# Early sums of the Fourier mixing moved ahead of the batch's end, and one operand of the two-level product formed a product earlier

## The chip, the cores and the metric

The kernel runs on one core of one Trainium2 chip, in fp32 throughout. The metric is the device time of one execution in microseconds (us). The engines are named as in the profile: PE is TensorE (matmuls and transposes), DVE is VectorE, ACT is ScalarE, POOL is GpSimd, SP issues most DMAs. PEld is the loading of weights, which runs beside the matmuls.

## The reference

Two blocks in a row. The first is attention over 8 batches x 8 heads, 576 positions, head size 64, in which only scores close to the row's maximum count:

```python
scores = scale * np.matmul(q, k.transpose(0, 1, 3, 2))
thresh = np.max(scores, axis=-1, keepdims=True) - tau
scores = np.where(scores >= thresh, scores, -1000000000.0)
attn = np.exp(scores - max); attn /= (sum + 1e-9)
x = attn @ v          # heads side by side: (8, 576, 512)
```

The second mixes every batch by a Fourier transform over both axes, keeps the real part, normalizes each row and runs it through two weight matrices:

```python
X = np.fft.fft(np.fft.fft(x, axis=1), axis=2)
u = x + np.real(X)
un = (u - mu) / np.sqrt(var + 1e-06)
ch = np.maximum(un @ w_ch1, 0.0) @ w_ch2     # 512 -> 2048 -> 512
return u + ch
```

## The kernel before

**Steps.** Attention goes by pairs of heads, four pairs to a batch, and by five query tiles to a pair, so a batch is 20 steps (`per_batch`) and the whole is 160. A step has scores on TensorE (L440, L446), the row maximum on DVE (`neg`, L520), the exponential on ACT (L526), a threshold (L530) and a masked sum on DVE (L540), and a scaling on ACT (L549). Transposes of the weights follow (`pe` L587, `pw` L605, copied from PSUM by ACT at L593 and L607), and products with v (`pv` L636, copied by ACT at L643). The loop over batches 2 to 7, which the change touches, starts at L1747 and writes out these pieces in a fixed order.

**Mixing.** The finished x of a batch is folded about its middle into `f` (L687 to L703; on DVE for the last pair, on POOL for the others). From the folds, sums and differences are formed that stand in for part of the transform. Some need only the first pairs of the batch: `fold_halves` (POOL) and `partial_sums` (DVE), a generator in three parts with 128 x 304 elements to an operation. Its first part is L729 and L730, its second part one `scaled` (L721) and its third two `scaled`. The rest is in `mixing(b)`, which the loop calls from step 2 of the next batch: the remaining sums (L751, L752, L754, L721), transforms over channels (`py` L766, copied by ACT into `y_e` and `y_o` at L771 and L776), transforms over positions (`pa` L783, L787) and additions into a ring of finished rows `u_t`.

The loop has `i` for the step. Before the change, at step 19 of a batch it creates the generator and runs its first part, behind the softmax's second third; it runs the second part further down in the same step. At the first step of the next batch it runs the third part, in the place where the first part stood. After the last step the third part stands behind the loop.

**Rows.** Finished rows go in nine groups of 512 through the two weight matrices. Group 0 is done plainly; groups 1 to 8 are `two_level(g, rows)`, a two-level Strassen scheme: seven products in place of eight, each of seven blocks. Its first half is `ph` (L1210) with sums on DVE (L1147) and ACT. Its second half has the products in the order `L1` = 1, 2, 5, 4, 6, 7, 3, at L1398, each in blocks `jn` 0 to 6. The left operands of the outer level are quadrants of the hidden layer (`a11`, `a12`, `a21`, `a22`) and combinations of them: product 1 reads `a11`, products 2 and 3 `a12`, product 5 and 6 `s1_tile`, product 4 `a22` and product 7 `a21`. Three of these are changed on the way by `l1_form`, in four parts of 128 x 512 at L1168: `a21 = a11 - a21` on POOL, `s1_tile -= a11` on DVE, and `a12 -= s1_tile` on POOL. The last one serves product 3, the last of the order, and reads the changed `s1_tile`.

The inner level needs four sums for each product, `l2_forms` (L1191): s1 and s2 on DVE, s3 and s4 on POOL, 128 x 512 each, formed while the product before runs. Product results come out of PSUM by an ACT copy (L1410) or a DVE addition (L1412, L1418), and are combined by POOL (`gather`, L1263) and DVE (`finish`, L895).

`at_slots(at, slots, jobs)` says behind which block `jn` of which product (index `at` in `L1`, from 0) a job is put on its engine's queue. Every engine runs its queue in order, and a job also waits for its inputs. While a softmax is being written out, such jobs are held back and follow it (`held`). `fill()` writes out as many blocks of the row groups as TensorE's budget for the step allows, so that products, attention and mixing lie beside each other. A group's rows are read back from `u_t` by `Rows.load` (`pn` L858, copies L863 and L864, statistics L869 and L870).

In the last group, 8, no attention runs any more. Its last two products are done plainly (L1377), and a `gather` addition of 128 x 896 on POOL (L1263) also lies behind block 1 of index 3.

PSUM is shared by all of this: four banks in a ring for everything but the scores (`po`, `ph`, `py`, `pa`, `pn`, `pe`, `pw`, `pv`) and two for the scores. A bank is free when its copy has run.

Of the kernel before, what the change touches and what calls it, by code (L numbers as in the profile page):

```python
# [47 lines left out]
def kernel(  # L48
# [378 lines left out]
    def scores(i):  # L427
        n, t = divmod(i, NT)
        qT, kT = heads[n][0:2]

        nh = 2 if t < 4 else 1
        sc = [ps.tile([128, 2, 512], FP32, tag="sc", name=f"sc{j}") for j in range(nh)]
        if t < 4:
            order = [(c, j) for c in range(2) for j in range(2)]
            if i < per_batch:
                order.sort(key=lambda cj: cj[1])
            for c, j in order:
                if True:
                    hp, k0 = slice(64 * j, 64 * j + 64), D * (1 - j)
                    nc.tensor.matmul(  # L440
                        sc[j][:, c, 0:HALF], qT[hp, 128 * t : 128 * t + 128],
                        kT[hp, k0 + HALF * c : k0 + HALF * (c + 1)], start=True, stop=True,
                    )
        else:
            for c in range(2):
                nc.tensor.matmul(  # L446
                    sc[0][:, c, 0:HALF], q_ends[:, :], kT[:, D + HALF * c : D + HALF * (c + 1)],
                    start=True, stop=True,
                )
        steps[i] = (sc, nh)  # L450
# [63 lines left out]
    def softmax_first(i):  # L514
        sc, nh = steps[i]
        neg = sb.tile([128, 2], FP32, tag="neg", bufs=3, name="neg")
        thr = sb.tile([128, 2], FP32, tag="thr", bufs=3, name="thr")
        e = sb.tile([128, 2 * S], FP32, tag="e", name="e")
        for j in range(nh):
            nc.vector.tensor_reduce(  # L520
                out=neg[:, j : j + 1], in_=sc[j][:, :, 0:HALF], axis=AXIS_XY, op=ALU.max,
                negate=True,
            )
        for j in range(nh):
            ej = e[:, S * j : S * (j + 1)].rearrange("p (c n) -> p c n", c=2)
            nc.scalar.activation(  # L526
                out=ej, in_=sc[j][:, :, 0:HALF], func=ACT.Exp, bias=neg[:, j : j + 1], scale=1.0
            )
            if j == 0:
                nc.scalar.activation(  # L530
                    out=thr[:, 0:nh], in_=neg[:, 0:nh], func=ACT.Identity,
                    bias=thr_off[:, :], scale=-1.0,
                )
        steps[i] = (sc, nh, e, thr)
# [185 lines left out]
    def scaled(out_, in0, factor, in1):  # L720
        nc.vector.scalar_tensor_tensor(  # L721
            out=out_, in0=in0, scalar=factor, in1=in1, op0=ALU.mult, op1=ALU.add
        )

    def partial_sums(b, eng=nc.vector):


        s = sums[b]
        eng.tensor_tensor(out=s[:, 0, E], in0=f[:, 0, E], in1=s[:, 1, E], op=ALU.add)  # L729
        eng.tensor_tensor(out=s[:, 0, O], in0=f[:, 0, O], in1=s[:, 1, O], op=ALU.subtract)  # L730
        yield
        scaled(s[:, 1, E], s[:, 1, E], flip, f[:, 0, E])
        yield
        scaled(f[:, 3, E], f[:, 3, E], minus, f[:, 0, E])
        scaled(f[:, 3, O], f[:, 0, O], plus, f[:, 3, O])
        yield
# [97 lines left out]
    def measure():  # L834
        while measures:
            measures.pop(0)()
# [257 lines left out]
    def quadrant(k, i):  # L1094
        return hs[:, 2048 * (2 * k + i) : 2048 * (2 * k + i + 1)]

    s1_tile = w1[3]
# [9 lines left out]
    def two_level(g, rows):  # L1107
# [52 lines left out]
        P, V = nc.gpsimd, nc.vector  # L1160
        a11, a12, a21, a22 = (quadrant(k, i) for i in range(2) for k in range(2))
# [3 lines left out]
        def l1_form(out_, in0, in1, engines):  # L1165
            def part(n, eng):
                c = slice(512 * n, 512 * n + 512)
                return lambda: eng.tensor_tensor(  # L1168
                    out=out_[:, c], in0=in0[:, c], in1=in1[:, c], op=ALU.subtract
                )  # L1170

            return [part(n, eng) for n, eng in enumerate(engines)]
# [97 lines left out]
        def gather(eng, v):  # L1270

            v = v.rearrange("p (j n) -> p j n", n=128)
            return [
                plus(eng, v[:, 1:5:3], twice(v[:, 0])),
                plus(eng, v[:, 5], v[:, 4]),
                plus(eng, v[:, 6], v[:, 2]),
                plus(eng, v[:, 6], v[:, 4]),
                plus(eng, v[:, 2:4], twice(v[:, 5])),
            ]
# [41 lines left out]
        def at_slots(at, slots, jobs):  # L1321
            for jn, job in zip(slots, jobs, strict=True):
                side.setdefault((at, jn), []).append(job)
# [12 lines left out]
        at_slots(1, (1, 2, 4, 6), l1_form(a21, a11, a21, (P, P, P, P)))  # L1336
        at_slots(2, (4, 5, 6), l1_form(s1_tile, s1_tile, a11, (V, V, V, V))[0:3])
        at_slots(3, (0,), l1_form(s1_tile, s1_tile, a11, (V, V, V, V))[3:4])
        at_slots(4, (1, 2, 4, 6), l1_form(a12, a12, s1_tile, (P, P, P, P)))
        at_slots(2, (0, 1, 2, 3, 4), gather(P, v_11))  # L1340
        at_slots(4, (2, 4), [lambda n=n: finish(0, 0, v_11)[n]() for n in range(2)])
        if not whole:
# [139 lines left out]
    per_batch = NPAIR * NT  # L1482
# [4 lines left out]
    def fill(hold=False, apart=False):  # L1487
        nonlocal budget, spent
        holding[:] = [True] if hold else []
        budget += per_slot  # L1490
        if mixes and not ended and not hold and not apart:
            mix(1)
        while work and spent < budget and work[0][0] < mixed:
            done = next(work[0][1], None)
            if done is None:
                work.pop(0)
            else:
                spent += done
        holding.clear()
        if mixes and ended:  # L1500
            mix(1)
# [124 lines left out]
    def fold_more():  # L1626
        if folds and next(folds[0], True):
            folds.pop(0)
# [16 lines left out]
    def mix(count):  # L1645
        nonlocal spent, mixed
        for _ in range(count):
            done = next(mixes[0], None)
            if done is None:
                mixes.pop(0)  # L1650
                mixed += 1
                break
            spent += done
# [93 lines left out]
    for i in range(2 * per_batch, total):  # L1747


        n, t = divmod(i, NT)  # L1750
        values = iter(())
        if i < total:
            scores(i)
        if t == 3 and i < total:
            values = values_in_parts(n, 0)
        elif t == 1 and n > 0:
            while folds:
                fold_more()
            values = values_in_parts(n - 1, 1)
        next(values, None)  # L1760
        if i % per_batch == 3:
            next(values, None)
        if i < total:
            softmax_first(i)
        next(values, None)
        if i % per_batch == 3:
            mix(1)
        if i % per_batch == 2:
            for _ in last_fold:
                pass  # L1770
            start_batch(i // per_batch - 1)
        fill(True)
        if i < total:
            softmax_second(i)
        measure()
        while held:
            held.pop(0)()
        if mixes:
            mix(1)
        if i % per_batch == 19:  # L1780
            partials = partial_sums(i // per_batch)
            next(partials)
        if i % per_batch == 0 and i > 2 * per_batch:
            next(partials)
        if t == 1:
            if n % NPAIR:
                folds.append(fold_rows(n - 1))
            else:
                last_fold = fold_rows(n - 1)
                next(last_fold)  # L1790
        weights = weights_in_parts(i - 1) if i <= total else iter(())
        next(weights, None)
        if t > 2 or i % per_batch == 17:
            fold_more()
        if i % per_batch == 19:
            next(partials)
        fill()
        if i % per_batch == 1:
            next(last_fold)
        next(weights, None)  # L1800
        if i < total:
            softmax_third(i)
            if t == 1:
                prep_ends(n)
            if t == 2 and n + 1 < B * NPAIR:
                scale_q(n + 1)
            if t == 3 and n + 1 < B * NPAIR:
                prep_pair(n + 1)
        if wanted:
            wanted.pop().factors()  # L1810
        if i % per_batch == 1:
            next(last_fold)
        fill(apart=i % per_batch == 2)
        if t == 2 and n + 1 < B * NPAIR:
            load_v(n + 1)
        if t == 4 and n + 2 < B * NPAIR:
            load_pair(n + 2)
    fill(True)
    while held:
        held.pop(0)()  # L1820
    next(partials)
    weights = weights_in_parts(total - 1)
    next(weights, None)
    fold_more()
# [83 lines left out]
```

## Time and profile before

| | us |
|---|---|
| median of 3 runs (1550.76 to 1551.69) | 1550.79 |
| profiled execution | 1552.55 |
| its span | 1550.8 |
| PE busy | 1523.1 (98%) |
| DVE busy | 1066.9 (69%) |
| ACT busy | 917.1 (59%) |
| POOL busy | 776.8 (50%) |

The span runs from the first instruction to the last; times in a timeline count from its start. A timeline line gives start, duration, engine, line, operation, output and inputs with their sizes, and after "x" the number of instructions of one kind drawn together; brackets at the end give the idle time before it and what ended it. The clock granted to TensorE was 1.00 over almost the whole span. The operations that the change moves, by their rows in the trace:

| line | engine | what | median, us | count |
|---|---|---|---|---|
| L729 | DVE | first early sum | 0.44 | 7 |
| L721 | DVE | scaled early sums | 0.53 | 32 |
| L1168 | POOL | a12 minus s1, one part | 1.34 | 32 |
| L1168 | DVE | s1 minus a11, one part | 0.68 | 32 |

The DVE part of L1168 stands at 470, 640, 810, 981, 1150, 1315, 1424 and 1519 us in groups 1 to 8, the a12 parts on POOL at 481, 650, 823, 992, 1162, 1327, 1432 and 1529.

### The profile page before, as it was taken

The numbers are of one execution on the slowest core, as the hardware profiler recorded it, in microseconds if no ns is written. First come the engines' busy times: TensorE is split into PE (matmuls) and PEld (weight loads), VectorE is DVE, ScalarE is ACT, GpSimd is POOL, SyncE is SP. The second block draws the span as 40 slices with busy tenths as digits, with TensorE's granted clock in tenths as the row PEclk, the third lists the DMA queues.
The fourth block names the chain that finished last, engine by engine and source line by source line (L and its number), as shares of the span: only waits on it lengthen the run. The fifth ranks groups of instructions, "written<-read, shape, count | busy, mean of one in ns | idle before, by whom it ended". The sixth has DMA issues, their size and how long they took to land.

```text
span 1550.8 us, 27036 instructions
## 1 busy us (share of the span) xinstructions
PE 1523.1 (98%) x9786; PEld 1185.1 (76%) x9786; DVE 1066.9 (69%) x2141; ACT 917.1 (59%) x1921; POOL 776.8 (50%) x964
## 2 busy tenths in 40 slices
PE   8999999999999999999999999999999999999999
PEld 5555555556788777877788778887788778989999
DVE  7987676846779466866588566956687666746546
ACT  6875675655656576656766666666666676232131
POOL 3775553034365643545254724555264626646635
PEclk9999999999999999999999999999999999999999
DMA  6423233465866344634464354635464534646655
GB/s 168 132 59 119 78 92 108 136 204 159 269 200 189 111 150 133 195 102 141 143 186 140 117 159 135 195 93 166 125 191 135 159 117 140 221 163 226 236 198 184
DMA packets 248907, 239.31 MB, mean 154 GB/s; under 512 B 197027, under 2 KB 218533, under 8 KB 228678
## 3 DMA queue, kind: packets, MB, share of 16 engines
q1 hardware_dynamic: 246262, 237.28, 50.1%
q8 instruction: 78, 1.28, 0.3%
q10 hardware_dynamic: 2512, 0.30, 0.1%
q14 instruction: 55, 0.45, 0.1%
HBM read 205.93 MB, written 31.46 MB: 153 GB/s over the span
## 4 chain that ended last, share of the span: by engine, by line
PE 84%; DVE 9%; ACT 3%; DMA 1%; POOL 1%; issue 1%; SPq 0%; ACTq 0%; DVEq 0%; POOLq 0%
PE ph L1210 25%; PE po L1398 18%; PE sc L440 9%; PE pv L636 9%; PE pw L605 7%; PE po L933 4%; PE ph L909 2%; PE sc L446 2%; PE py L766 2%; PE pa L783 1%; PE pe L587 1%; PE pa L787 1%; PE pm L360 1%; PE po L1377 1%; PE pn L858 1%
## 5 line engine op out<-in xcount | busy, mean ns | idle before, releaser
L520 DVE TENSOR_REDUCE neg<-sc 128x1 f32<-128x576 f32 x216 | 154.2, 750 | 113.0 <-PE sc L440 99.6
L526 ACT ACTIVATE e<-sc,neg 128x576 f32<-128x576 f32 x216 | 158.6, 734 | 121.6 <-DVE neg L520 121.5
L1147 DVE TENSOR_TENSOR hs<-ph,hs 128x512 f32<-128x512 f32 (+1 forms) x128 | 105.4, 823 | 168.0 <-PE ph L1210 97.7
L1398 PE MATMUL po<-w,w_all 128*128 128x128 f32 x1728 | 219.4, 276 | 0.3 <-ACT ends L593 0.3
L1398 PEld LDWEIGHTS po<-w,w_all 128*128 128x128 f32 x1728 | 205.0, 192 | 9.4 <-issue 4.0
L1156 POOL TENSOR_TENSOR w<-hs 128x512 f32<-128x512 f32 x32 | 42.1, 1317 | 313.8 <-ACT hs L1152 240.0
L540 DVE SCALAR_TENSOR_TENSOR e<-sc,thr,e 128x576 f32<-128x576 f32 x216 | 168.3, 812 | 20.6 <-ACT thr L530 20.6
L1210 PE MATMUL ph<-u_t,w 128*128 128x256 f32 x768 | 180.9, 382 | 0.5 <-DMA w<-f 0.5
L440 PE MATMUL sc<-kT,qT 64*128 64x288 f32 x1024 | 169.8, 431 | 7.1 <-DVE e L477 6.1
L607 ACT COPY e_t<-pw 128x512 f32<-128x512 f32 x256 | 148.6, 595 | 44.1 <-PE pw L605 42.7
L605 PE MATMUL pw<-ident,e 128*128 128x128 f32 x1152 | 168.8, 273 | 6.0 <-ACT ends L593 1.9
L549 ACT ACTIVATE e<-e,den 128x576 f32<-128x576 f32 x216 | 157.4, 775 | 8.9 <-DVE den L388 8.2
L1210 PEld LDWEIGHTS ph<-u_t,w 128*128 128x128 f32 x768 | 140.9, 190 | 23.6 <-issue 5.3
L1210 PE MATMUL ph<-w_all,w 128*128 128x256 f32 x672 | 157.1, 382 | 1.1 <-DVE w_all L1132 1.0
L605 PEld LDWEIGHTS pw<-ident,e 128*128 128x128 f32 x1152 | 134.8, 141 | 21.9 <-issue 5.6
L1152 ACT ACTIVATE hs<-hs 128x512 f32<-128x512 f32 (+1 forms) x96 | 74.1, 772 | 114.5 <-DVE hs L1147 113.7
L1210 PEld LDWEIGHTS ph<-w_all,w 128*128 128x128 f32 x672 | 123.4, 190 | 23.9 <-issue 4.9
L440 PEld LDWEIGHTS sc<-kT,qT 64*128 64x128 f32 x1024 | 96.3, 187 | 57.1 <-issue 23.7
L1263 POOL TENSOR_TENSOR w_all<-w_all 128x128 f32<-128x128 f32 (+2 forms) x160 | 118.4, 757 | 29.1 <-DVE w_all L1418 20.2
L1398 PE MATMUL po<-w,hs 128*128 128x128 f32 x912 | 120.0, 278 | 0.3 <-ACT ends L593 0.3
L1398 PEld LDWEIGHTS po<-w,hs 128*128 128x128 f32 x912 | 109.9, 192 | 9.9 <-issue 8.0
L593 ACT COPY ends<-pe 128x128 f32<-128x128 f32 (+1 forms) x128 | 38.1, 298 | 58.7 <-PE pe L587 40.1
(227 smaller groups left out, 2945.3 us busy)
## 6 DMA issues: line engine op xcount, KB each, us to landing
w<-f SPq DMA_DIRECT2D x150, 1024.0 KB, 4.9
hs<-in_moe_w_ch_dram SPq DMA_DIRECT2D x23, 512.0 KB, 4.7
q_in<-in_q_dram SPq DMA_DIRECT2D x128, 72.0 KB, 4.3
out_dram<-u SPq DMA_DIRECT2D x36, 256.0 KB, 2.5
k_in<-in_k_dram SPq DMA_DIRECT2D x124, 72.0 KB, 2.4
v_in<-in_v_dram SPq DMA_DIRECT2D x64, 128.0 KB, 5.0
f<-w SPq DMA_DIRECT2D x14, 512.0 KB, 3.3
f<-w SPq DMA_DIRECT2D x7, 1024.0 KB, 4.8
```

The lines of the kernel that those rows point to most:

```text
L440: nc.tensor.matmul(sc[j][:, c, 0:HALF], qT[hp, 128 * t : 128 * t + 128], kT[hp, k0 + HALF * c : k0 + HALF * (c + 1)], start=True, stop=True,)
L520: nc.vector.tensor_reduce(out=neg[:, j : j + 1], in_=sc[j][:, :, 0:HALF], axis=AXIS_XY, op=ALU.max, negate=True,)
L526: nc.scalar.activation(out=ej, in_=sc[j][:, :, 0:HALF], func=ACT.Exp, bias=neg[:, j : j + 1], scale=1.0)
L540: nc.vector.scalar_tensor_tensor(out=ej, in0=sc[j][:, :, 0:HALF], scalar=thr[:, j : j + 1], in1=ej, op0=ALU.is_ge, op1=ALU.mult, accum_out ...
L549: nc.scalar.activation(out=e[:, S * j : S * (j + 1)], in_=e[:, S * j : S * (j + 1)], func=ACT.Copy, scale=den[:, j : j + 1],)
L605: nc.tensor.transpose(pw[:, c, :], e[:, c0 : c0 + 128], ident[:, :])
L607: nc.scalar.copy(e_t[:, 4 * j : 4 * j + 4, qs], pw[:, :, :])
L636: nc.tensor.matmul(pv[64 * j : 64 * j + 64, 0:m], vt[:, 2 * c + j, :], e_t[:, 4 * j + c, 0:m] if c < 4 else ends[:, 0, 0:m], start=(c == 0 ...
L1147: nc.vector.tensor_tensor(out=to, in0=bank, in1=to if other is None else other, op=ALU.add)
L1210: nc.tensor.matmul(bank[:, 256 * q : 256 * q + 256].rearrange("p (two n) -> p two n", two=2), left[:, 256 * c + 128 * q : 256 * c + 128 * ...
L1263: return lambda: eng.tensor_tensor(out=to, in0=to, in1=other, op=ALU.add)
L1398: nc.tensor.matmul(to, lefts[m][j][:, s], right_[:, 128 * s : 128 * (s + 1)], start=jn in (0, 4) and s == 0, stop=s == 3, skip_group_check ...
```

## The change

The generator of early sums is created at the end of step 18, behind that step's last `fill`, and runs its first part there. In step 19 the place that was the first part's now runs the second (one `scaled`), and the place that was the second part's, just ahead of a `fill`, runs the third (two `scaled`), which stood in the first step of the next batch before. The call behind the loop goes. The four parts of `a12 -= s1_tile` go from behind blocks 1, 2, 4 and 6 of the fifth product in the order (index 4) to the same blocks of the fourth (index 3). The numbers of instructions on every engine and the order of TensorE's stay as they were. In the last group the first a12 part now stands on POOL's queue ahead of the 128 x 896 addition, the others between the fourth product's inner sums.

```diff
@@ -1336,7 +1336,7 @@
         at_slots(1, (1, 2, 4, 6), l1_form(a21, a11, a21, (P, P, P, P)))
         at_slots(2, (4, 5, 6), l1_form(s1_tile, s1_tile, a11, (V, V, V, V))[0:3])
         at_slots(3, (0,), l1_form(s1_tile, s1_tile, a11, (V, V, V, V))[3:4])
-        at_slots(4, (1, 2, 4, 6), l1_form(a12, a12, s1_tile, (P, P, P, P)))
+        at_slots(3, (1, 2, 4, 6), l1_form(a12, a12, s1_tile, (P, P, P, P)))
         at_slots(2, (0, 1, 2, 3, 4), gather(P, v_11))
         at_slots(4, (2, 4), [lambda n=n: finish(0, 0, v_11)[n]() for n in range(2)])
@@ -1778,9 +1778,6 @@
         if mixes:
             mix(1)
         if i % per_batch == 19:
-            partials = partial_sums(i // per_batch)
-            next(partials)
-        if i % per_batch == 0 and i > 2 * per_batch:
             next(partials)
         if t == 1:
             if n % NPAIR:
@@ -1811,6 +1808,9 @@
         if i % per_batch == 1:
             next(last_fold)
         fill(apart=i % per_batch == 2)
+        if i % per_batch == 18:
+            partials = partial_sums(i // per_batch)
+            next(partials)
         if t == 2 and n + 1 < B * NPAIR:
             load_v(n + 1)
@@ -1818,7 +1818,6 @@
     fill(True)
     while held:
         held.pop(0)()
-    next(partials)
     weights = weights_in_parts(total - 1)
```

## The prediction

> **What bounds the kernel now.** I read the busy shares first, then the chain that ended last, then TensorE's waits, then the timelines of the engines around the two places that the change touches.
>
> ```profile
> PE 1523.1 (98%) x9786; PEld 1185.1 (76%) x9786; DVE 1066.9 (69%) x2141; ACT 917.1 (59%) x1921; POOL 776.8 (50%) x964
> ...
> PE 84%; DVE 9%; ACT 3%; DMA 1%; POOL 1%; issue 1%; SPq 0%; ACTq 0%; DVEq 0%; POOLq 0%
> ```
>
> TensorE is busy 98% of the span. The change gives it no work and takes none, so time can only be won where it waits now, and lost where it would wait anew. Its waits between 800 and 1200 us, in us, number and longest:
>
> ```profile
> PE py L766 <- ACT y_e L776: 2.0, 3, 0.7
> PE pw L605 <- ACT w_all L1410: 1.5, 1, 1.5
> ```
>
> The three of 0.67 come after batch ends; smaller ones stand at 497.20 (0.19) and 656.35 (0.29), and one of 1.06 at 664.93, all behind DVE operations that wait for POOL's a12 parts. That is all I see to win: 3 x 0.67 + 0.19 + 0.29 + 1.06 = 3.55 us.
>
> Now VectorE (DVE) and then GpSimd (POOL) in one group's fourth and fifth product, about 981 to 1002 us:
>
> ```profile
> 981.25 0.66 DVE L1168 TENSOR_TENSOR w<-w,hs 128x512 f32<-128x512 f32 x1
> 981.82 0.97 DVE L721 SCALAR_TENSOR_TENSOR f<-f,factors 128x304 f32<-128x304 f32 x2
> 982.71 1.89 DVE L1168 TENSOR_TENSOR w<-w,hs 128x512 f32<-128x512 f32 x3
> 984.71 0.69 DVE L1191 TENSOR_TENSOR w_all<-w 128x512 f32<-128x512 f32 x1
> 985.31 1.42 DVE L520 TENSOR_REDUCE neg<-sc 128x1 f32<-128x576 f32 x2
> ...
> 991.89 3.14 DVE L692 TENSOR_TENSOR f<-half 128x143 f32<-128x143 f32 x4
> ...
> 997.47 1.77 DVE L1191 TENSOR_TENSOR w_all<-w_all,hs 128x512 f32<-128x512 f32 x1
> ```
>
> ```profile
> 987.14 1.32 POOL L1191 TENSOR_TENSOR w_all<-w 128x512 f32<-128x512 f32 x1 [7.94 <-PE po L1398]
> ...
> 992.14 2.72 POOL L1168 TENSOR_TENSOR hs<-hs,w 128x512 f32<-128x512 f32 x2
> 996.19 1.27 POOL L1191 TENSOR_TENSOR w_all<-hs 128x512 f32<-128x512 f32 x1 [1.33 <-PE po L1398]
> 997.42 1.28 POOL L1168 TENSOR_TENSOR hs<-hs,w 128x512 f32<-128x512 f32 x1
> ```
>
> The four L692 take 3.14 us in place of 4 x 0.30: two of them, beside POOL's L1168, take 1.37 each. L1191 at 997.47 takes 1.77 in place of 0.68, beside the L1168 at 997.42. L520, which reads PSUM, keeps its 0.75. So a DVE operation with two SBUF inputs waits out a POOL tensor_tensor (about 1.25 us from start to start), and the two engines then take turns. I count with that.
>
> **Place one: the early sums.** Per batch, L729 and L730 (0.44 and 0.47 us in five of seven batches) move from step 19 to the end of step 18; two L721 (0.89 us from start to start) move from the next batch's first step to step 19. Nothing is added in sum, and no DMA moves.
> - End of step 18, typical group (966 to 980): DVE comes free after the L1412 at 966.54, and POOL works without a gap from 965.25 to 970.46 (L1191, L1168 in turn). L729 and L730 each wait for one POOL operation, so the L520 at 968.84 starts about 0.86 late. What it feeds, e at L526, has TensorE work in front of it: no wait of PE.
> - Step 19: three L721 (3 x 0.445) replace L729, L730 and one L721 (1.19 from first start to last end). DVE's L1191 comes later by that and lets POOL's L1191 (released at 974.33) go ahead. At the L520 of 976.78 DVE is 0.8 late.
> - First step: 0.89 less before the L520 of 985.31.
> - First group (455 to 460): L729 before the L1412 of 457.31 makes that 1.0 later (L729 took 1.10 there, beside POOL). TensorE's L1398 at 458.10 waits for it: +1.0. In the third group (807.07) the existing wait of 1.52 grows by 0.97 for the same reason.
>
> **Place two: a12 during the fourth product.** Each of POOL's four a12 parts waits only for its own part of DVE's L1168 (s1 minus a11). Before, POOL was idle for 7.94 us up to 987.14 and took the parts from 992. Now the first part is released when the first DVE part ends, 0.6 us after 981.25, and DVE's other three are still to come. In turns: DVE's second part, POOL's first, DVE's third, POOL's second, DVE's fourth. Two DVE parts wait 1.25 each: +2.5. With 0.8 from place one and 0.89 saved, the L520 of 985.31 starts 2.42 late.
>
> Who waits for it? ACT runs in order:
>
> ```profile
> 986.16 0.74 ACT L526 ACTIVATE e<-sc,neg 128x576 f32<-128x576 f32 x1 [4.14 <-DVE neg L520]
> ...
> 987.61 0.42 ACT L643 COPY x<-pv 128x320 f32<-128x320 f32 x1
> ```
>
> ```profile
> 988.23 0.27 PE L587 MATMUL pe<-ident,e 128*128 128x128 f32 x1
> 988.34 0.60 PE L605 MATMUL pw<-ident,e 128*128 128x128 f32 x4
> ```
>
> The pv copy L643 is queued behind both exponentials and ends at 988.03. It empties one of the ring's four banks, and the pw at 988.34 takes that one. Slack 0.31. A start 2.42 later makes PE wait 2.1. The same order with the same slack stands at 646 (copy 645.96 + 0.42, pw 646.69) and at 1157 (1156.76, 1157.48). At 810 PE has already waited in front of this (slack 1.9): about +0.3 in all there with place one and less 0.67. In the groups without softmax (1316, 1424) no PE wait follows: GpSimd's fourth sum is due 0.6 us before it is needed.
>
> What the move frees: no a12 parts from 992 to 1002, some 3 us of waiting on DVE (two L692 1.08 each, L1191 1.1, L895). The later L721 and y_e come earlier, and the 3.55 us of old waits go.
>
> **The last group.** POOL, 1518 to 1535:
>
> ```profile
> 1522.04 2.53 POOL L1263 TENSOR_TENSOR w_all<-w_all 128x896 f32<-128x896 f32 x1
> 1524.53 1.72 POOL L1191 TENSOR_TENSOR w_all<-w 128x512 f32<-128x512 f32 x1
> 1527.76 1.27 POOL L1191 TENSOR_TENSOR w_all<-w,w_all 128x512 f32<-128x512 f32 x1 [1.51 <-DVE w_all L1191]
> 1528.98 6.19 POOL L1168 TENSOR_TENSOR hs<-hs,w 128x512 f32<-128x512 f32 x4
> ```
>
> Three a12 parts (1.25 each) now stand in front of the second L1191 (sum s4 for product 6), which ended at 1529.03. POOL's gap of 1.51 pays for some; DVE's two L1191 and its 896-wide L1263 take turns with the parts. Walked in turns, from 1522.6: a12 1523.85, DVE 1524.5, L1263 1526.5, DVE 1527.2, a12 1528.45, DVE 1529.1, L1191 1530.35, DVE 1531.4, a12 1532.7, L1191 about 1534.0. TensorE's blocks that read it start at 1531.79: +2.2, right at the end with nothing behind to take it up. No turn-taking: three parts less the gap leave it ready near 1531, no wait. These are the bounds, 0 and +2.3; I take the upper, as the L1168 of 1522.55 on DVE shows the same exclusion there (2.57 us beside L1263).
>
> **Sum**, us: first group +1.0 - 0.2 = +0.8; second +2.1 - 1.06 - 0.29 = +0.75; third +0.3; fourth +2.1 - 0.67 = +1.4; fifth the same +1.4; sixth and seventh 0; last +2.25. Total +6.9. The profiled execution took 1552.55 us, 1.76 above the median of the three runs; the sum on the median gives 1557.7.
>
> The wait at 985 is bounded below by 0 (POOL starts after DVE's fourth part) and above by 3.35: POOL's L1191 of 987.14, released by PE, and DVE's second L1191 start within 0.01 us of each other, and whichever comes second waits 1.25 more. I take 2.1, without that.
>
> The Trainium skill ("SBUF — State Buffer", the summary of rules for kernel authors) says that a DVE operation with two SBUF inputs and a GpSimd operation reading SBUF exclude each other fully, and that one should run whichever is off the critical path; that speaks against putting POOL's parts beside DVE's. Its section on the bandwidth intuition adds some 115 ns at a hand-over; estimated from that page, four hand-overs would make a group's delay 0.46 longer. The trace shows none: two alternating L692 start 1.30 apart, and POOL's operation is 1.24 to 1.28 of it.
>
> **The rivals.**
> - *Worse: a turn lost too.* At 987 POOL's L1191 gets in first in the second, fourth and fifth groups (3 x 1.25), and the y_e waits stay, their cause lying on ACT (3 x 0.67): 1557.7 + 3.75 + 2.0 = 1563.5. For it: the 0.01 us. Against: DVE's long rows just before each y_e wait.
> - *No change: L643 is not what pw waits for.* The bank is freed in time, PE keeps its order: 6.9 - 3 x 2.1 = +0.6, 1551.4. For it: the slack is read from one bank order and the trace names no such wait now. Against: pw starts 0.31 after the copy ends.
> - *Faster, the other side: these pairs don't exclude each other.* Parts of L1168 on both engines run side by side from 981.9, place one costs nothing, the last sum is ready at 1531, and DVE loses its company at 992: -3.55, 1547.2. It decides if DVE's L1168 keep under about 0.9 us on average. For it: L1168 of 982.71 and other DVE rows at full speed while POOL idles say nothing of it. Against: L692, L1191, L1168 at 1522.55 all stretched.
>
> **How the numbers follow.** Base case 0.52, worse 0.16, no change 0.14, faster 0.18. A difference of 0.2% (3.1 us) is about what a measurement here can tell. Range: low end 1549, which leaves out most of the faster case; high end 1563, which leaves out half of the worse one. Faster by over 3.1 us is 0.16 of the faster case's 0.18; within it, the no-change case's 0.14, 0.02 from faster and 0.03 from a base case whose tail bound is 0; the rest, 0.65, is slower.
>
> **What would show it.** Right: DVE's L1168 parts with a mean of 1.3 us or more; a PE wait "pw L605" behind L643's bank of about 2 at 647, 989 and 1159; a wait of L1398 for POOL's L1191 of about 2.2 near 1532; one of L1398 of 1.0 at 458; no y_e waits; L692 all at 0.3. Wrong: pw starting on time though the L520 is late; POOL's a12 parts beside DVE's with neither stretched; or, in the last group, a PE that does not wait.

## The result and the profile after

| | before | after |
|---|---|---|
| median of 8 runs, us | 1550.99 (1549.65 to 1554.14) | 1554.68 (1552.78 to 1557.31) |
| ratio to before | | 1.0023, 95% interval 1.0013 to 1.0034 |
| span of the profiled execution, us | 1550.8 | 1554.9 |
| PE / DVE / ACT / POOL busy, us | 1523.1 / 1066.9 / 917.1 / 776.8 | 1526.5 / 1076.5 / 914.2 / 786.1 |

The changed kernel is slower by 0.23%, 3.7 us; the forecast was 6.9. The runs of one kernel spread by some 5 us, and the long ones are those with the lower mean clock granted to TensorE: of 28 runs of the kernel before beside the first experiments, the three at 1.000 took 1549.1 to 1549.8 us, the ten at 0.998 1551.8 to 1553.8, the one at 0.996 1555.9. DVE and POOL show some 10 us more of busy time each with the same instructions: an operation that is held on its engine counts as busy (POOL's L1191 of 976.01 below shows 2.02 us in place of 1.27).

TensorE's waits over the whole run, after the change (us in all, times, longest), those that matter here:

```profile
PE pw L605 <- ACT x L643: 2.6, 3, 0.9
...
PE pw L605 <- ACT w_all L1410: 1.8, 1, 1.8
...
PE po L1398 <- POOL w_all L1191: 1.2, 1, 1.2
...
PE py L766 <- ACT y_e L776: 0.9, 5, 0.2
...
PE po L1398 <- DVE w_all L1412: 0.7, 1, 0.7
```

And the same view before, for the lines that differ past 450 us, where the changed code runs:

```profile
PE py L766 <- ACT y_e L776: 2.4, 5, 0.7
...
PE pw L605 <- ACT w_all L1410: 1.5, 1, 1.5
PE pw L605 <- DVE w_all L1418: 1.1, 1, 1.1
```

Three waits are new: for L643 (three times), for POOL's L1191 and for DVE's L1412, one each. One has grown, two have shrunk or gone. All were in the forecast; most are smaller than it said. Now the place around 983 us, on DVE, POOL, ACT and PE of the changed kernel:

```profile
976.21 0.69 DVE L1191 TENSOR_TENSOR w_all<-hs 128x512 f32<-128x512 f32 x1
...
978.50 1.41 DVE L520 TENSOR_REDUCE neg<-sc 128x1 f32<-128x576 f32 x2
...
982.95 4.62 DVE L1168 TENSOR_TENSOR w<-w,hs 128x512 f32<-128x512 f32 x4
987.67 0.69 DVE L1191 TENSOR_TENSOR w_all<-w 128x512 f32<-128x512 f32 x1
988.28 1.42 DVE L520 TENSOR_REDUCE neg<-sc 128x1 f32<-128x576 f32 x2
989.62 1.02 DVE L1191 TENSOR_TENSOR w_all<-w_all,w 128x512 f32<-128x512 f32 x1
```

```profile
976.01 2.02 POOL L1191 TENSOR_TENSOR w_all<-hs 128x512 f32<-128x512 f32 x1 [1.32 <-PE po L1398]
...
983.69 3.33 POOL L1168 TENSOR_TENSOR hs<-hs,w 128x512 f32<-128x512 f32 x2 [2.82 <-DVE w L1168]
```

```profile
989.13 0.74 ACT L526 ACTIVATE e<-sc,neg 128x576 f32<-128x576 f32 x1 [5.43 <-DVE neg L520]
...
990.58 0.42 ACT L643 COPY x<-pv 128x320 f32<-128x320 f32 x1
```

```profile
989.90 0.27 PE L587 MATMUL pe<-ident,e 128*128 128x128 f32 x1
991.05 0.66 PE L605 MATMUL pw<-ident,e 128*128 128x128 f32 x4 [0.88 <-ACT x L643]
```

DVE's four L1168 take 4.62 us where four at 0.60 from start to start and 0.08 more for the last one's end would be 2.5: two of them take 1.76 each, beside the two a12 parts that POOL starts at 983.69. The L520 behind them feeds the exponentials, L643 stands behind both, and pw starts 1.15 after the transpose L587 ahead of it; before, it was 0.11 (988.23 and 988.34). So 1.04 is lost here, and the same 1.04 at 649.60 and 1160.74.

TensorE runs the same 9786 matmuls and transposes in the same order in all kernels of this study, so each can be set against its counterpart and a loss be put on one instruction. From 450 us on, where the changed code runs, the changed kernel's order falls back by 3.19 us in its profiled execution; ahead of that, where no instruction of the change stands, the eleven other profiles end between 3.2 us earlier and 1.0 later than the kernel before.

### The profile page after: what moved, and what is told of

The parts are those of the page before. It is cut to its first block, busy times and chain, and to the rows that moved or that the text cites. A ratio compares the mean times of both kernels' runs of the same rounds, so it can differ in the third digit from the quotient of the medians.

```text
span 1554.9 us, 27021 instructions
## 1 busy us (share of the span) xinstructions
PE 1526.5 (98%) x9786; PEld 1186.0 (76%) x9786; DVE 1076.5 (69%) x2141; ACT 914.2 (59%) x1921; POOL 786.1 (51%) x964
## 4 chain that ended last, share of the span: by engine, by line
PE 86%; DVE 5%; ACT 3%; POOL 3%; issue 2%; DMA 0%; POOLq 0%; ACTq 0%; DVEq 0%
PE ph L1210 24%; PE po L1398 19%; PE pv L636 10%; PE sc L440 9%; PE pw L605 7%; PE po L933 4%; PE ph L909 3%; PE sc L446 2%; PE py L766 2%; PE pd L111 1%; PE pa L783 1%; PE pe L587 1%; PE pa L787 1%; PE pm L360 1%; PE po L1377 1%
## 5 line engine op out<-in xcount | busy, mean ns | idle before, releaser
L520 DVE TENSOR_REDUCE neg<-sc 128x1 f32<-128x576 f32 x216 | 154.2, 751 | 106.9 <-PE sc L440 99.6
L1398 PE MATMUL po<-w,w_all 128*128 128x128 f32 x1728 | 219.9, 277 | 2.2 <-POOL w_all L1191 1.2
L1398 PEld LDWEIGHTS po<-w,w_all 128*128 128x128 f32 x1728 | 205.1, 192 | 11.6 <-issue 4.5
L540 DVE SCALAR_TENSOR_TENSOR e<-sc,thr,e 128x576 f32<-128x576 f32 x216 | 168.3, 812 | 22.3 <-ACT thr L530 22.1
L1398 PE MATMUL po<-w,hs 128*128 128x128 f32 x912 | 120.0, 278 | 0.3 <-ACT ends L593 0.3
L1398 PEld LDWEIGHTS po<-w,hs 128*128 128x128 f32 x912 | 109.9, 192 | 9.9 <-issue 8.0
L1191 POOL TENSOR_TENSOR w_all<-hs 128x512 f32<-128x512 f32 x38 | 54.0, 1421 | 43.8 <-PE po L1398 43.7
```

The costliest lines, as they stand in the source:

```text
L520: nc.vector.tensor_reduce(out=neg[:, j : j + 1], in_=sc[j][:, :, 0:HALF], axis=AXIS_XY, op=ALU.max, negate=True,)
L540: nc.vector.scalar_tensor_tensor(out=ej, in0=sc[j][:, :, 0:HALF], scalar=thr[:, j : j + 1], in1=ej, op0=ALU.is_ge, op1=ALU.mult, accum_out ...
L1398: nc.tensor.matmul(to, lefts[m][j][:, s], right_[:, 128 * s : 128 * (s + 1)], start=jn in (0, 4) and s == 0, stop=s == 3, skip_group_check ...
```

## The experiments

Each kernel was run beside the kernel before on the same chip. "In the trace" means the shift of TensorE's order against the kernel before, from 450 us to the end, in one profiled execution each. A wait for a DMA at 1451 us (0.3 to 0.6 in these kernels) alone shifts it by up to 0.25 one way or the other.

**One part alone.** The sums as changed, a12 as before:

```diff
-        at_slots(3, (1, 2, 4, 6), l1_form(a12, a12, s1_tile, (P, P, P, P)))
+        at_slots(4, (1, 2, 4, 6), l1_form(a12, a12, s1_tile, (P, P, P, P)))
```

> The early sums as in the changed kernel, a12 during the fifth product as before. My theory: this part alone costs the late L1412 in the first group (0.84 us in the changed kernel's trace) and a little at 808 (0.24), and wins nothing: the waits of py for y_e stay at 0.67 and the one at 665 at 1.06, and there is no wait of pw for L643, since the L520 in question comes earlier, not later. About +1.1 us on the kernel before, 1552.1. Rival, the sums carry the whole loss: 1554 or more. Rival, the sums are hidden wholly: 1551.0.

Ratio to before 1.0007 (0.9998 to 1.0016); in the trace +1.07. The two steps are 0.84 at 457 and 0.25 at 808, and y_e's waits and the one at 665 are as before. By the trace the sums cost a microsecond and win nothing; the times alone do not tell this kernel from the one before.

And a12 as changed, the sums as before (the diff's first part alone):

> a12 during the fourth product as in the changed kernel, the early sums where they were before. My theory: the L520 behind DVE's L1168 parts starts 2.1 late and not 1.3, as the 0.89 us that the two L721 take away from in front of it are not saved; pw waits for L643 about 1.85 instead of 0.88, in three groups; the waits for y_e fall to 0.18, the one at 665 to 0.1, and the last group loses 1.4. Sum +5.5 - 1.5 - 1.0 + 1.4 = +4.4, 1555.4. Rival, the wait for L643 has nothing to do with where the L721 stand: 0.88 stays, and the whole is +1.6 to +2, 1552.8.

Ratio 1.0026 (1.0015 to 1.0038), about 4.0 us; in the trace +4.60. Its waits:

```profile
PE pw L605 <- ACT x L643: 5.0, 3, 1.7
...
PE po L1398 <- POOL w_all L1191: 1.2, 1, 1.2
...
PE py L766 <- ACT y_e L776: 0.9, 5, 0.2
```

The wait for L643 is 1.68 each and not 0.88 (1.84 in TensorE's order, against 1.04). So the two parts don't add: the sums' move takes 0.89 us from in front of that L520 and so halves the harm that the a12 move does there. Alone, it has nothing to halve.

**The last group.** The changed kernel with a12 at the old place in group 8 only:

```diff
-        at_slots(3, (1, 2, 4, 6), l1_form(a12, a12, s1_tile, (P, P, P, P)))
+        at_slots(4 if whole else 3, (1, 2, 4, 6), l1_form(a12, a12, s1_tile, (P, P, P, P)))
```

> The changed kernel, but in the last group a12 stands behind the fifth product again. My theory: only the wait of L1398 for POOL's L1191 near 1535 goes (1.2 us idle, 1.37 in TensorE's order), 1.4 us less than the changed kernel, 1553.3. Rival, something else ends the last group: time as in the changed kernel, 1554.7.

Ratio 1.0011 (1.0002 to 1.0020), against 1.0023 with the whole change. In the trace +1.88 against +3.19; the only step of more than 0.15 us in which its order differs from the changed kernel's past 450 us is that of L1398 in the last group, 1.37. That wait is the a12 parts' doing.

**The order on ACT.** The changed kernel with pv's copy ahead of the exponentials in the batch's second step:

```diff
-        if i % per_batch == 3:
+        if i % per_batch in (1, 3):
             next(values, None)
```

> The changed kernel, but in the second step of each batch the copy of pv (L643) is put on ACT ahead of the two exponentials instead of behind them. Nothing else moves. My theory: what L643 waits for is the queue: it now runs as soon as pv is done (by 988.1, before the row maximum), and pw starts on time; the three waits of 0.88 go, 1.04 each in TensorE's order, and 3.1 us with them: 1551.6. Rival, the wait passes to the next copy behind the exponentials (L1410), whose bank TensorE wants next: 1554.7.

Ratio 1.0012 (1.0003 to 1.0021); in the trace +2.52, so 0.7 better than the changed kernel and not 3.1. Both theories have a share. ACT and PE:

```profile
983.91 0.43 ACT L643 COPY x<-pv 128x320 f32<-128x320 f32 x1 [3.99 <-PE pv L636]
985.34 0.74 ACT L526 ACTIVATE e<-sc,neg 128x576 f32<-128x576 f32 x1 [1.00 <-DVE neg L520]
...
986.78 0.58 ACT L1410 COPY w_all<-po 128x512 f32<-128x512 f32 x1
```

```profile
986.12 0.27 PE L587 MATMUL pe<-ident,e 128*128 128x128 f32 x1
986.23 0.60 PE L605 MATMUL pw<-ident,e 128*128 128x128 f32 x4
987.42 2.05 PE L1398 MATMUL po<-w,w_all 128*128 128x128 f32 x16 [0.59 <-ACT w_all L1410]
```

L643 runs 1.4 us ahead of the first exponential, and pw starts on time (1.04 gone): the queue was what L643 waited for. But the next bank of the ring is emptied by L1410, which still stands behind the exponentials, and 0.76 of the 1.04 comes back half a microsecond later. That leaves 0.28 three times; 0.26 of it goes again in the second group, where py now waits for y_e. Moving one copy out of the queue does not mend it; the late L520 has to go.

**Earlier, but behind DVE's parts.** The kernel before with a12 in the fourth product at its end:

```diff
-        at_slots(4, (1, 2, 4, 6), l1_form(a12, a12, s1_tile, (P, P, P, P)))
+        at_slots(4 if whole else 3, (1, 2, 4, 6) if whole else (4, 5, 6, 6), l1_form(a12, a12, s1_tile, (P, P, P, P)))
```

> The kernel before, but in groups 1 to 7 the four a12 parts stand behind blocks 4, 5, 6 and 6 of the fourth product: still a product earlier than before, but on POOL's queue behind the inner sum s3, which waits for TensorE till past DVE's four L1168 parts. The last group and the early sums are as before. My theory: the harm of the earlier place is its meeting with DVE's L1168 ahead of the row maximum, not its being earlier. So DVE's parts stay at 0.68, no wait of pw for L643 comes up, and the wins stay: y_e 3 x 0.49 and most of 0.97 at 665. About -2.4 us on the kernel before, -0.15%. Rival, the wins of the changed kernel need POOL free by 988 and are lost here: 0. Second rival, any earlier a12 delays POOL's s4 and TensorE waits for it: slower, +1 or more.

Ratio 0.9992 (0.9983 to 1.0002); in the trace -1.86. No wait for L643, the three y_e waits down by 0.49 each, the one at 665 down by 0.97; 0.2 is lost again at 829 and 998 each, and some 0.7 near 1454. The direction is that of my theory; by its times alone this kernel is not told from the one before (its runs had a mean granted clock of 0.9977, those of the kernel before 0.9985, which by the spread above I estimate to be worth about 1 us).

The same with the changed sums:

> The same late place of a12 in groups 1 to 7 and the old one in the last group, with the early sums of the changed kernel. My theory: the sums cost their 0.84 in the first group and 0.25 at 808 here too and win nothing, so 1.1 us more than with the old sums: -1.3 us on the kernel before. Rival, with the L643 wait gone the two L721 taken out of the batch's first step pay: equal to or faster than with the old sums.

Ratio 1.0001 (0.9992 to 1.0010), in the trace +0.32. That is 2.2 more than with the old sums. The 0.84 and 0.24 are there, and a third, unforeseen, of 1.14 at 1168, where pw waits for L593. That copy stands behind the exponentials, and they wait for a late row maximum. What makes it late is a lost turn. DVE and POOL with the changed sums:

```profile
1158.76 2.99 DVE L687 TENSOR_TENSOR half<-x 128x287 f32<-128x287 f32 x2
...
1163.73 1.76 DVE L1191 TENSOR_TENSOR w_all<-hs 128x512 f32<-128x512 f32 x1
1165.41 1.41 DVE L520 TENSOR_REDUCE neg<-sc 128x1 f32<-128x576 f32 x2
```

```profile
1158.71 1.27 POOL L1191 TENSOR_TENSOR w_all<-w,w_all 128x512 f32<-128x512 f32 x1
```

and with the old ones:

```profile
1157.54 1.87 DVE L687 TENSOR_TENSOR half<-x 128x287 f32<-128x287 f32 x2
...
1161.40 1.75 DVE L1191 TENSOR_TENSOR w_all<-hs 128x512 f32<-128x512 f32 x1
1163.07 1.41 DVE L520 TENSOR_REDUCE neg<-sc 128x1 f32<-128x576 f32 x2
```

```profile
1157.55 1.55 POOL L1191 TENSOR_TENSOR w_all<-w,w_all 128x512 f32<-128x512 f32 x1
```

DVE's L1191 is held alike in both (1.76 and 1.75), so it is not the difference. The difference is L687: POOL's L1191 starts 0.05 us ahead of it with the changed sums and goes first, and 0.01 behind it with the old ones and goes second. In TensorE's order the L520 is 1.12 later for it. This 1.14 hangs on 0.06 us and came in one of three groups; whether every run has it is not shown.

**What excludes.** Three variants, each with POOL's a12 parts replaced in the changed kernel: by memsets of a12, by memsets of s1, and by copies.

```diff
-        at_slots(3, (1, 2, 4, 6), l1_form(a12, a12, s1_tile, (P, P, P, P)))
+        at_slots(3, (1, 2, 4, 6), [lambda n=n: P.memset(a12[:, 512 * n : 512 * n + 512], 0.0) for n in range(4)])
```

> The changed kernel, but POOL's four a12 parts are memsets of the same 128 x 512 pieces, in the same places: the subtraction of a12 is left out, so that product 3 has a zero operand. Theory: DVE's two-input L1168 is held because POOL's operation reads SBUF. Then all four DVE parts take 0.66 to 0.70, the row maximum behind them starts 2.1 earlier, and pw does not wait for L643. Rival, it is held by any POOL work on these tiles, writes too: two of four parts stay at 1.7 or at 0.68 plus the memset's own time, and the wait for L643 remains.

DVE's parts took 0.66 to 0.68 at 980 and no wait for L643 was left; in the trace -1.63 (one run, 1550.46). But here the two did not meet: the first two memsets need nothing of DVE and ran at 978.10 and 978.56, ahead of its first part at 980.24. At this place it says only that without the meeting there is no harm. Elsewhere in the same trace they do meet. The fourth memset runs beside DVE's four L692, which have two SBUF inputs too. DVE and POOL:

```profile
990.87 0.99 DVE L692 TENSOR_TENSOR f<-half 128x143 f32<-128x143 f32 x4
```

```profile
991.11 0.53 POOL L1339 MEMSET hs<- 128x512 f32 x1
```

None of the four is stretched (0.29 to 0.34 each; beside the subtraction two took 1.37 each in the kernel before). In the first, sixth and seventh group the second memset also ran beside one of DVE's L1168 (at 470.76, 1316.71 and 1425.57), and that one took 0.68. So a POOL operation that only writes does not hold DVE's.

```diff
+        at_slots(3, (1, 2, 4, 6), [lambda n=n: P.memset(s1_tile[:, 512 * n : 512 * n + 512], 0.0) for n in range(4)])
```

> The changed kernel, but each of POOL's four a12 parts is a memset of the part of s1_tile that DVE's L1168 has just written: it is released by the same DVE part, meets the next one as a12 did, and reads nothing. The subtraction of a12 is left out and product 6 has a zero operand. Theory, the exclusion needs a POOL operation that reads SBUF: all four DVE parts stay at 0.66 to 0.70, POOL's memsets at about 0.53, and pw does not wait for L643. Rival, any POOL access excludes: two DVE parts grow by a memset's 0.5, to about 1.2, or the memsets wait for DVE's parts to end.

This was to mend that and did not: the memset also waits until DVE's L1191 has read the part (it ran at 982.62, past all four L1168). TensorE then waited for the memsets in the last groups (4.9 us), so the one time, 1558.36, says nothing of the change. Beside L692 (its fourth memset, 990.17) the picture is the same as above: 0.29 to 0.34 each.

```diff
+        at_slots(3, (1, 2, 4, 6), [lambda n=n: P.tensor_copy(a12[:, 512 * n : 512 * n + 512], s1_tile[:, 512 * n : 512 * n + 512]) for n in range(4)])
```

> The changed kernel, but each of POOL's four a12 parts copies the part of s1_tile that DVE's L1168 has just written into a12: one operand read in place of two, the subtraction left out (product 3 reads s1 minus a11 there). Theory, one read is enough to exclude: two DVE parts take 0.68 plus the copy's own 0.6 or so, some 1.2 to 1.3, and pw waits for L643 by what that adds beyond the slack, 0 to 0.3. Rival, only two-input POOL operations exclude: DVE's parts stay at 0.68.

Here they met. DVE and POOL:

```profile
979.25 3.29 DVE L1168 TENSOR_TENSOR w<-w,hs 128x512 f32<-128x512 f32 x4
982.64 0.69 DVE L1191 TENSOR_TENSOR w_all<-w 128x512 f32<-128x512 f32 x1
983.25 1.41 DVE L520 TENSOR_REDUCE neg<-sc 128x1 f32<-128x576 f32 x2
```

```profile
979.97 2.02 POOL L1339 COPY hs<-w 128x512 f32<-128x512 f32 x2 [2.80 <-DVE w L1168]
```

Four parts in 3.29 us: two of them took 1.09, that is 0.41 more than 0.68. With the subtraction it was 1.07 more, with nothing beside it 0. So, with the memset's zero, it is POOL's reading that counts, one read is enough, and the wait grows with POOL's operation (a copy takes 0.60 alone, a subtraction 1.27). No wait for L643 was left, as the two turns lost (0.83) are what the moved sums save (0.89): the L520 at 983.25 is on time in TensorE's order. The trace is at -1.60 (one run, 1549.46).

**A version that beats both.** As with the late place above, but in groups 1 to 6 only:

```diff
-        at_slots(4, (1, 2, 4, 6), l1_form(a12, a12, s1_tile, (P, P, P, P)))
+        at_slots(4 if g > 6 else 3, (1, 2, 4, 6) if g > 6 else (4, 5, 6, 6), l1_form(a12, a12, s1_tile, (P, P, P, P)))
```

> The kernel before with a12 behind blocks 4, 5, 6 and 6 of the fourth product in groups 1 to 6 only; groups 7 and 8 and the early sums as before. In the trace with the late place to group 7, TensorE lost 0.5 near 1454 behind L1132, which the old place of group 7 does not. My theory: the wins stay (3 x 0.49 and 0.97) and this 0.5 does not come up: -2.4 us on the kernel before, ratio 0.9984, clear of 1. Rival: the 0.5 comes from elsewhere and stays, -2.0.

Median 1549.10, ratio 0.9985 (0.9976 to 0.9994): faster than before, by 2.3 us going by the ratio and by 1.7 going by the medians (1550.77 before); in the trace -2.22, and the loss near 1454 does not come up. POOL and DVE in the same stretch as above:

```profile
984.50 1.32 POOL L1191 TENSOR_TENSOR w_all<-w 128x512 f32<-128x512 f32 x1 [7.94 <-PE po L1398]
...
986.58 1.27 POOL L1168 TENSOR_TENSOR hs<-hs,w 128x512 f32<-128x512 f32 x1
```

```profile
980.07 1.89 DVE L1168 TENSOR_TENSOR w<-w,hs 128x512 f32<-128x512 f32 x3
...
982.67 1.41 DVE L520 TENSOR_REDUCE neg<-sc 128x1 f32<-128x576 f32 x2
```

The first a12 part now starts 4 us behind DVE's L1168 and behind the row maximum that matters.

## Why the prediction was right in direction and too high by 3 us

The base case happened: the changed kernel is slower, at the places named and by the chain named. Term by term, us, by steps in TensorE's order:

| place | forecast | measured |
|---|---|---|
| first group: L1412 behind L729 and L730 | +1.0 | +0.84 |
| first group: wait at 497 | -0.2 | 0 |
| third group: L1410 at 808 | +0.97 | +0.24 |
| L643 in the second, fourth, fifth group | 3 x 2.1 | 3 x 1.04 |
| wait at 665 | -1.06 | -0.97 |
| wait at 656 | -0.29 | 0 |
| y_e, three waits | 3 x -0.67 | 3 x -0.49 |
| fifth group, gap at 1158 | not counted | -0.19 |
| last group: POOL's L1191 | +2.25 | +1.37 |
| steps too small to list | | +0.25 |
| sum | +6.9 (rounded by group) | +3.2 |

- **The wait for L643 was mis-sized by half, in two terms.** The first is the 0.8 us of lateness that place one was to hand down through step 19 (in the third group, at 808, the 0.97). It rested on POOL's L1191 getting ahead of DVE's. It didn't: POOL's, due at 976.01, took 2.02 us, being held until DVE's L1191 of 976.21 was done. The L520 at 978.50 was 0.04 late against TensorE's order there, not 0.8. In the third group, with no lost turn either, 0.24 was left: 0.12 from three L721 in place of L729, L730 and one L721 (1.31 against 1.19), and 0.12 from an L540 that came late behind the moved L729 and L730.
- **The second is the price of a turn.** I took POOL's start-to-start time, 1.25, as what a DVE operation loses. The traces show 1.07 (1.76 against 0.68). The row was in my own text: the L692 lost 1.08 each. Two turns are 2.15, less 0.89 saved and 0.04 more is a lateness of 1.30; pw's slack took 0.25. With a12 alone moved nothing is saved: the L520 (at 986.69) is 2.09 late, and 1.84 are lost, again 0.25 less.
- **The last group** was walked with the same price, about 1.9 for a POOL and a DVE operation of 512 in turn; two such pairs took 1.68. The four pairs between the first a12 part and s4 were walked at 8.85 and took 7.93, which is the 0.9 by which the walk was late. The place and the cause were right.
- **The old waits** fell as said, but y_e keeps 0.18 each time: that is the ACT copy itself (0.63 at L771, then L776; in the changed kernel it starts as soon as py is done), which no freed DVE shortens. I had taken the whole wait as DVE's. The 0.19 at 497 is that same remainder, and the 0.29 at 656 is a wait for L593 that stays as it was. "No a12 parts from 992 to 1002" did not hold either: the fourth part starts at 995.01, and one L692 beside it still takes 1.38.
- **The rivals.** "A turn lost too" hung on a near tie that rested on the lateness of 2.42: DVE's L1191 of 984.71, due at 987.13, against POOL's at 987.14. With a lateness of 1.30 there was no tie (DVE 987.67, POOL 988.82). That it stayed away is the mis-sized term at work, not something that I had reasoned. The next L1191 of DVE did lose part of a turn (1.02 at 989.62), but it stands behind both L520, so nothing before the exponentials moved. "L643 is not what pw waits for" fell by the wait lines, and by pw's start on time when L643 was put first; the ring's next bank then showed that L643 is not alone. "These pairs don't exclude each other" fell by the L1168 lines, and by the copy, which cost DVE less as it is shorter.
- **Two readings** were off without weight in the sum. POOL had a gap of 0.20 (at 967.77) in the stretch called without one, and the 1.19 us of the early sums in step 19 run to the start of the next operation, not to their last end (1.27).

The rule that I had set against the change, from the Trainium skill ("SBUF — State Buffer", the summary of rules for kernel authors), that the two-input DVE operation and the reading POOL operation exclude each other, agrees with all of this: 1.76, 1.09 and 0.68 us beside a subtraction, a copy and a memset. The extra 115 ns of the section on the bandwidth intuition, which that page measured on a DMA whose descriptors GpSimd writes, is not seen between these operations; the DVE operation loses 0.2 less than POOL's takes.

## What to carry to other kernels

Forming an operand earlier on an idle engine is not free when its operation excludes another engine's: look at what stands right behind the operations that it will meet, here the row maximum on which ACT's queue and, through two PSUM banks, TensorE depend. The same work a few blocks later, behind that maximum, kept the gain and lost the cost (with the old sums -1.9 us in the trace in place of +4.6, of which 1.4 are the last group's, where the old place was kept). Price a turn by a stretched row of the operation that waits, not by the length of the one it waits for, and don't mend such a delay by reordering one copy: the next bank of the ring waits for the next copy in the queue.

## What the runs showed of the hardware that was not expected

A DVE operation with two SBUF inputs loses about 0.19 us less than the POOL operation beside it takes: 1.07 beside 1.27 (subtraction) and 0.41 beside 0.60 (copy). With both queues full, the one whose operation was issued first does not always go first: POOL's L1191, which counts from 976.01, let DVE's L1191 of 976.21 through. In two nearer ties the one that started first did go first (POOL by 0.05 at 1158.71, DVE by 0.01 at 1157.54). Which of the two wins was read wrongly at 976, and what decides it is not settled by these runs. A POOL operation that only writes (memset, 0.53) cost DVE's nothing.
